# One branch for two groups of products, with up to four widths, in the first mixture of experts

## The chip, the core and the metric

The kernel runs on one core of a Trainium2 chip. Its engines work side by side and wait for each other through semaphores: TensorE (PE; its weight loads are shown as PEld), VectorE (DVE), ScalarE (ACT), GpSimd (POOL) and SyncE (SP). The metric is the device time of one execution in microseconds (us). The median of three runs before the change is 817.31 us (816.48 to 819.75).

## The reference

The kernel computes a chain of three layers in float32. The first is windowed attention (4 batches, 8 heads, 576 positions, head width 64). The second is a mixture of 8 experts over 2304 tokens, in which each token goes to the one expert that its gate picks. The third is a dense layer with a softplus. The second layer is where the change lies:

```
logits = x @ w_gate
e_idx = np.argmax(logits, axis=1)
...
for e in range(E):
    mask = e_idx == e
    h = np.maximum(x[mask] @ w1[e], 0.0)
    ye = h @ w2[e]
    out[mask] = gate_w[mask, None] * eom[mask, e, None] * ye
```

Here x is 2304x512, w1[e] is 512x1024 and w2[e] is 1024x512. How many tokens an expert gets is known only when the kernel runs.

## The kernel before, in words

Up to about 160 us the kernel does attention and the gate. Then it goes through the experts one after the other, as "ranks" 0 to 7 (`for r in range(NE)`, L1309): rank 0 is the expert that leads after the first 11 of 20 token tiles, and ranks 1 to 7 are the others by falling count. The second dense layer follows from about 396 us.

Each rank has a fixed capacity of columns (tokens), CAPS = 424, 392, 344, 328, 312, 288, 280, 256. Tokens beyond a capacity are done by `overflow()`, a block that all engines run past between rank 0 and rank 1; with the reference's inputs none is left over. Working out the reference's gate on its inputs gives 356, 370, 312, 309, 280, 278, 203 and 196 tokens for ranks 0 to 7.

A rank has 16 steps, u = 0 to 15. In steps 0 to 7, `up` computes one block of 128 hidden rows each (tile ph, with ReLU by ACT into hh and the rest hl by DVE). In steps 8 to 15, `down` computes four blocks of 128 output rows (tile py), each in two halves. A float32 product is split into high and low parts, so each term is three matmuls (wh xh, wh xl, wl xh). A group is the 12 matmuls of one `up` or of one half of a `down`; a rank has 16 groups, 192 matmuls.

PE, ACT, DVE and SP take their instructions in the order in which the code writes them (`manual_schedule`). In a step stand also, in this order: gathering and transposing the next rank's tokens (`gather_tr`, PE transposes into px, L855, two buffers), splitting a weight piece into its high and low part (`hi_` on ACT, `lo_` on DVE), and then `up` or `down`. The weights come by DMA (tile wr); a new load is issued by SP as soon as `lo_` has freed a buffer.

Matmuls need not run over the whole capacity. `mm3_r` (L871) reads the rank's token count from a register of PE and branches: if the count is at most the rank's cut in CUTS (L26), the group runs over the cut's columns (L890 to L892; the first matmul of an accumulation stays as wide as the capacity), else over the capacity (L894 to L896). Rank 0 has no branch. Each group has its own branch, and both forms ("arms") stand in PE's program one behind the other.

Of the kernel before, what the change touches and what calls it, by code (L numbers as in the profile page):

```python
# [11 lines left out]
F32 = mybir.dt.float32  # L12
# [9 lines left out]
P = 128  # L22

MASKED = 1.0e30
ROWS_AT = 8
CUTS = [(), (344,), (320,), (304,), (288,), (264,), (256,), (240,)]  # L26
RB = 5
WARM = 28
NE_AT = ((6, 14), (7, 0), (7, 1), (7, 2))
# [13 lines left out]
def attn_moe_softplus_kernel(ctx: ExitStack, tc: tile.TileContext, q, k, v, w_gate, w_ogate, w1, w2, w_in, w_out, out, dbg=None):  # L43
    nc = tc.nc
    B, H, S, D = q.shape
    NT, DM = out.shape
    NE = w_gate.shape[1]
# [6 lines left out]
    NC = DM // P  # L54
# [24 lines left out]
    tabi = const.tile([1, 40], I32, name="tabi")  # L79
# [453 lines left out]
    K = {"rt": rt_p, "ixe": const}  # L533
# [292 lines left out]
    def part(r, j, c, n, fs):  # L826
        return [t.rearrange("p (c f) -> p c f", c=n)[:, c, fs] for t in pieces[r, j][-2:]]
# [38 lines left out]

    rows_val = {}

    def mm3_r(r, n, ps, terms, *a):
        if r not in rows_val:  # L870
            mm3(ps[:, :n], [(w, [x[:, :n] for x in xs_]) for w, xs_ in terms], *a)  # L871
            return

        def arms(cuts):
            if not cuts:
                mm3(ps[:, :n], [(w, [x[:, :n] for x in xs_]) for w, xs_ in terms], *a)
                return
            with tc.If(rows_val[r] <= cuts[0]) as c:
                mm3(ps[:, :n], [(w, [x[:, :n] for x in xs_]) for w, xs_ in terms], *a, cut=cuts[0])
            with c.Else():  # L880
                arms(cuts[1:])

        arms(CUTS[r])

    def mm3(ps, terms, first=True, last=True, cut=None):
        k = len(terms)
        for i, ((wh, wl), (xh, xl)) in enumerate(terms):
            if cut:
                wide = first and i == 0
                nc.tensor.matmul(ps if wide else ps[:, :cut], wh, xh if wide else xh[:, :cut], start=wide, stop=False, skip_group_check=True)  # L890
                nc.tensor.matmul(ps[:, :cut], wh, xl[:, :cut], start=False, stop=False, skip_group_check=True)  # L891
                nc.tensor.matmul(ps[:, :cut], wl, xh[:, :cut], start=False, stop=(last and i == k - 1), skip_group_check=True)  # L892
                continue
            nc.tensor.matmul(ps, wh, xh, start=(first and i == 0), stop=False)  # L894
            nc.tensor.matmul(ps, wh, xl, start=False, stop=False)  # L895
            nc.tensor.matmul(ps, wl, xh, start=False, stop=(last and i == k - 1))  # L896

    hT = {}

    def up(r, n, f):  # L900
        xh, xl = xs[r]
        pool, tag = K["ph"]
        ps = pool.tile([P, 512], F32, tag=tag, name=f"ph{r}_{f}")
        fs = slice(P * (f % 2), P * (f % 2) + P)
        mm3_r(r, n, ps, [(part(r, f // 2, c, 4, fs), (xh[:, c], xl[:, c])) for c in range(NC)])
        hh, hl = [K["hh"].tile([P, CW], F32R, tag=t, name=f"{t}{r}_{f}") for t in ("hh", "hl")]
        nc.scalar.activation(hh[:, :n], ps[:, :n], AF.Relu)
        nc.vector.scalar_tensor_tensor(hl[:, :n], ps[:, :n], 0.0, hh.bitcast(F32)[:, :n], ALU.max, ALU.subtract)
        hT[r, f] = (hh[:, :n], hl[:, :n])

    yps = {}
# [9 lines left out]
                tc.declare_no_dep(ywr[r, o].ins, ld.ins, reason="this rank lies behind the columns read")  # L921

    def down(r, n, o, half, off, eng):
        if half == 0:
            yps[r, o] = K["py"][0].tile([P, 512], F32, tag=K["py"][1], name=f"py{r}_{o}")
        ps = yps[r, o]
        os_ = slice(P * o, P * o + P)
        fs = range(4 * half, 4 * half + 4)
        mm3_r(r, n, ps, [(part(r, 4 + f // 2, f % 2, 2, os_), hT[r, f]) for f in fs], half == 0, half == 1)
        if half == 1:  # L930
            store_y(r, n, o, ps, off, eng)

    NL = GROUPS[G_DRAM][1]
    xacc = {}
# [301 lines left out]
        K[key] = (bctx.enter_context(tc.tile_pool(name=nm, bufs=bufs, space=PSUM)), nm)  # L1239
    def overflow():  # L1240
        total = nc.values_load(tabi[0:1, 4 * NE : 4 * NE + 1], min_val=0, max_val=NT // OVW)
        with tc.If(total > 0):


            with tc.For_i(0, NE) as r:
                left = nc.values_load(tabi[0:1, ds(r + 3 * NE, 1)], min_val=0, max_val=NT // OVW)
                with tc.For_i(0, left) as kw:
                    e_, o_, c_ = [
                        nc.sync.value_load(tabi[0:1, ds(r + i * NE, 1)], min_val=0, max_val=m)
                        for i, m in ((0, NE - 1), (1, NT), (2, NT))  # L1250
                    ]
                    t0 = nc.s_assert_within(c_ - kw * OVW - OVW, min_val=0, max_val=NT - OVW, skip_runtime_bounds_check_because="an overflow window ends at its expert's last token")
                    y0 = nc.s_assert_within(o_ + t0, min_val=0, max_val=NT - OVW, skip_runtime_bounds_check_because="an overflow window ends at its expert's last token")
                    load_idx("v", e_ * NT + t0, OVW)
                    for t in range(ntile(OVW)):
                        gather("v", OVW, t)
                    for j in range(4):
                        load_piece("v", j, e_)
                        piece_hi("v", j)
                        piece_lo("v", j)  # L1260
                    for t in range(ntile(OVW)):
                        for fn in (gather_scale, gather_tr, gather_hi, gather_lo):
                            fn("v", OVW, t)
                    for f in range(NF1):
                        up("v", OVW, f)
                    for j in range(4, 8):
                        load_piece("v", j, e_)
                        piece_hi("v", j)
                        piece_lo("v", j)
                    for o in range(NC):  # L1270
                        for half in range(2):
                            down("v", OVW, o, half, y0, nc.sync)
# [43 lines left out]
    for r in range(NE):  # L1316
        n = CAPS[r]
        if r == 1:
            sched.close()
            overflow()  # L1320
            mctx.enter_context(tc.manual_schedule(engines=manual))
        off = tab_load(nc.scalar, NE + r, NT) if r else 0
        perm_off = tab_load(nc.sync, NE + r, NT) if r else 0
        nc.sync.dma_start(perm_dram[ds(perm_off, NT)], idx_dram[ds(er[r] * NT, NT)])
        for u in range(16):

            if r == 0:
                next(ordering, 0)
                if u == ROWS_AT:
                    loaded = nc.values_load_multi_w_load_instructions(tabi[0:1, 2 * NE + 1 : 3 * NE], engines=[nc.tensor.engine])[1]  # L1330
                    rows_val.update({k_ + 1: v_ for k_, v_ in enumerate(loaded)})
                if u == 4:
                    K["ranked"] = True
                    er[1] = tab_load(nc.sync, 1, NE - 1)
                    load_idx(1, er[1] * NT, CAPS[1])
                    nload[1] -= 1
                    load_next()
            if r + 2 < NE:
                if u == IDX_AT:
                    if r + 2 not in er:  # L1340
                        er[r + 2] = tab_load(nc.sync, r + 2, NE - 1)
                    load_idx(r + 2, er[r + 2] * NT, CAPS[r + 2])
                if 0 <= u - GATHER_AT < ntile(CAPS[r + 2]):
                    gather(r + 2, CAPS[r + 2], u - GATHER_AT)
            if r + 1 < NE:
                m = CAPS[r + 1]
                if r == 0 and 0 <= u - 6 < ntile(m):
                    gather(r + 1, m, u - 6)
                for s, fn in zip((9, 10, 11, 12) if r == 0 else TR_AT, (gather_scale, gather_tr, gather_hi, gather_lo)):
                    if 0 <= u - s < ntile(m):  # L1350
                        fn(r + 1, m, u - s)

            if r < NE - 1 or u < 8:
                k_ = (r, 4 + u // 2) if u < 8 else (r + 1, (u - 8) // 2)
                (hi_, lo_)[u % 2](*k_)
            if r == NE - 1:
                for fn, *a in last_rank.get(u, ()):
                    fn(*a)
            if (r, u) in NE_AT:
                load_piece(NE, NE_AT.index((r, u)))  # L1360
            if r == NE - 1:
                if u in X2_AT:
                    x2_load(X2_AT.index(u))
            if r and u % 5 == 0:
                prep_tick(new_b, NPREP, 3)
            if u < 8:
                up(r, n, u)
            else:
                down(r, n, (u - 8) // 2, u % 2, off, nc.scalar)
# [154 lines left out]
```

## Time and profile before

| what | value |
|---|---|
| median of 3 runs | 817.31 us (816.48 to 819.75) |
| the profiled execution, its own time | 819.59 us |
| its span, first to last instruction | 818.0 us |
| PE matmul busy | 773.8 us, 95% |
| PE weight loads busy | 694.5 us, 85% |
| DVE / ACT / POOL busy | 566.6 / 471.8 / 144.6 us |
| ranks 0 to 7 | about 160 to 396 us |
| mean granted clock of PE | 0.986 |

All times in the profile are of one execution. A matmul's shown duration holds its passage through the array, so back-to-back matmuls overlap in the timeline; what one costs the stream is the distance between the starts.

### The profile page before, as it was taken

The numbers are of one execution on the slowest core, as the hardware profiler recorded it, in microseconds if no ns is written. First come the engines' busy times: TensorE is split into PE (matmuls) and PEld (weight loads), VectorE is DVE, ScalarE is ACT, GpSimd is POOL, SyncE is SP. The second block draws the span as 40 slices with busy tenths as digits, with TensorE's granted clock in tenths as the row PEclk, the third lists the DMA queues.
The fourth block names the chain that finished last, engine by engine and source line by source line (L and its number), as shares of the span: only waits on it lengthen the run. The fifth ranks groups of instructions, "written<-read, shape, count | busy, mean of one in ns | idle before, by whom it ended". The sixth has DMA issues, their size and how long they took to land.

```text
span 818.0 us, 14909 instructions
## 1 busy us (share of the span) xinstructions
PE 773.8 (95%) x5542; PEld 694.5 (85%) x5543; DVE 566.6 (69%) x1112; ACT 471.8 (58%) x909; POOL 144.6 (18%) x170
## 2 busy tenths in 40 slices
PE   6898886999999999999989999999999999999994
PEld 5666664898999999999978887899999999999993
DVE  5767885663667877756799999866656666766662
ACT  4675642344556666566766666656656655655561
POOL 9824343121002012100011222120001001001001
PEclk9999998799999999999999999999999999999998
DMA  9997665255788898669432312220001001001000
GB/s 209 264 243 186 144 159 154 59 193 182 233 275 277 304 299 279 213 216 320 135 103 78 104 53 83 70 85 1 20 0 40 1 1 39 1 0 40 1 1 38
DMA packets 85879, 104.36 MB, mean 128 GB/s; under 512 B 30428, under 2 KB 61404, under 8 KB 85792
## 3 DMA queue, kind: packets, MB, share of 16 engines
q1 hardware_dynamic: 74496, 84.22, 35.7%
q0 software_dynamic: 5104, 13.40, 4.9%
q10 hardware_dynamic: 6192, 5.56, 2.0%
q8 instruction: 57, 0.93, 0.5%
q14 instruction: 30, 0.25, 0.1%
HBM read 83.98 MB, written 19.32 MB: 126 GB/s over the span
## 4 chain that ended last, share of the span: by engine, by line
PE 59%; DVE 12%; issue 9%; ACT 4%; DMA 2%; POOL 1%; POOLq 0%; ACTq 0%; SPq 0%; DVEq 0%
PE pg L895 5%; PE pg L896 5%; PE pg L894 5%; PE q L1433 5%; PE q L1432 5%; PE q L1431 5%; PE ph L894 3%; PE ph L896 3%; PE py L894 3%; PE ph L895 3%; PE py L895 2%; PE py L896 2%; DVE l L1411 2%; PE py L890 2%; PE py L891 2%
## 5 line engine op out<-in xcount | busy, mean ns | idle before, releaser
L895 PE MATMUL pg<-xlm,wh 128*128 128x384 f32 x384 | 129.7, 338 | 0.0
L896 PE MATMUL pg<-xhm,wl 128*128 128x384 f32 x384 | 129.4, 337 | 0.0
L894 PE MATMUL pg<-xhm,wh 128*128 128x384 f32 x384 | 129.4, 337 | 0.0
L1433 PE MATMUL q<-wh,gl 128*128 128x512 f32 x288 | 114.2, 397 | 3.8 <-DVE gl L732 3.8
L1431 PE MATMUL q<-wh,gh 128*128 128x512 f32 x288 | 114.2, 396 | 1.3 <-ACT gh L1417 0.9
L1432 PE MATMUL q<-wl,gh 128*128 128x512 f32 x288 | 113.3, 393 | 0.0
L732 DVE TENSOR_TENSOR wl<-wr,wh 128x1024 fp32r<-128x1024 f32 x72 | 87.6, 1219 | 33.3 <-ACT wh L787 33.3
L1417 ACT CAST gh<-l 128x384 fp32r<-128x384 f32 x96 | 49.2, 513 | 100.5 <-DVE l L1411 100.5
L732 DVE TENSOR_TENSOR gl<-l,gh 128x384 fp32r<-128x384 f32 x96 | 56.6, 590 | 41.3 <-ACT gh L1417 40.2
L787 ACT CAST wh<-wr 128x1024 fp32r<-128x1024 f32 x72 | 75.0, 1047 | 15.2 <-ACT y L917 6.7
L894 PEld LDWEIGHTS pg<-xhm,wh 128*128 128x128 f32 x384 | 72.2, 188 | 3.9
L895 PEld LDWEIGHTS pg<-xlm,wh 128*128 128x128 f32 x384 | 72.1, 188 | 3.8
L1433 PEld LDWEIGHTS q<-wh,gl 128*128 128x128 f32 x288 | 54.1, 188 | 21.9 <-DVE gl L732 10.2
L1402 DVE TENSOR_SCALAR w<-u 128x384 f32<-128x384 f32 x96 | 34.7, 361 | 54.6 <-ACT u L1400 53.9
L896 PEld LDWEIGHTS pg<-xhm,wl 128*128 128x128 f32 x384 | 72.2, 188 | 0.0
L1440 POOL DMA_INDIRECT out_dram<-o,perm_sb x18 | 18.6, 1033 | 271.9 <-DVE o L259 137.4
L1411 DVE TENSOR_TENSOR l<-l,u 128x384 f32<-128x384 f32 x96 | 62.2, 648 | 2.8
L1431 PEld LDWEIGHTS q<-wh,gh 128*128 128x128 f32 x288 | 54.1, 188 | 11.7 <-ACT gh L1417 4.2
L1432 PEld LDWEIGHTS q<-wl,gh 128*128 128x128 f32 x288 | 54.1, 188 | 8.2
L1399 ACT ACTIVATE u<-pg 128x384 f32<-128x384 f32 x96 | 46.9, 489 | 22.9 <-PE pg L896 22.5
L837 POOL DMA_INDIRECT xg<-x_dram,idx x25 | 29.9, 1198 | 167.7 <-ACT wh L787 79.0
L1404 DVE SCALAR_TENSOR_TENSOR u<-w,u 128x384 f32<-128x384 f32 x96 | 53.5, 557 | 2.8
(205 smaller groups left out, 1806.8 us busy)
## 6 DMA issues: line engine op xcount, KB each, us to landing
wr<-in_moe_w_dram SPq DMA_DIRECT2D x64, 512.0 KB, 5.4
raw<-in_q_dram SPq DMA_DIRECT2D x8, 576.0 KB, 7.0
raw<-in_k_dram SPq DMA_DIRECT2D x8, 576.0 KB
x2r<-yT_dram SPq DMA_DIRECT2D x12, 384.0 KB, 4.6
vP<-in_v_dram SPq DMA_DIRECT2D x16, 272.0 KB, 10.8
praw<-in_moe_w_in_dram SPq DMA_DIRECT2D x8, 512.0 KB
praw<-in_moe_w_out_dram SPq DMA_DIRECT2D x8, 512.0 KB, 5.8
wr<-in_moe_w_in_dram SPq DMA_DIRECT2D x8, 512.0 KB
```

Of the source, the lines that this page charges most:

```text
L732: e.tensor_tensor(lo, src, hi.bitcast(F32), ALU.subtract)
L787: (eng or nc.scalar.copy)(d[1], d[0])
L894: nc.tensor.matmul(ps, wh, xh, start=(first and i == 0), stop=False)
L895: nc.tensor.matmul(ps, wh, xl, start=False, stop=False)
L896: nc.tensor.matmul(ps, wl, xh, start=False, stop=(last and i == k - 1))
L1399: nc.scalar.activation(u, ps, AF.Abs)
L1404: nc.vector.scalar_tensor_tensor(u, w_, 1.0, u, ALU.subtract, ALU.subtract)
L1411: nc.vector.tensor_tensor(l, l, u, ALU.subtract)
L1417: nc.scalar.copy(gT[b, f][0], l)
L1431: nc.tensor.matmul(acc[b, t], gh[:, ts_], wh, start=(f == 0), stop=False)
L1432: nc.tensor.matmul(acc[b, t], gh[:, ts_], wl, start=False, stop=False)
L1433: nc.tensor.matmul(acc[b, t], gl[:, ts_], wh, start=False, stop=(f == NF - 1))
```

## The change

Three edits, all of which act on PE's program.

1. `mm3_r` takes several groups and puts one branch around them. `up` now issues the groups of steps f and f+1 together in the even step, and `down` both halves together in its first step (the second step only stores).
2. CUTS gets up to three cuts for a rank, tried in rising order, so that four forms of each pair of groups stand in the program. Rank 0 gets cuts too: the register load moves from step 8 to step 10 of rank 0 and now holds rank 0's count, so its outputs o = 1 to 3 (the last six groups) branch.
3. The overflow test is turned round (`total <= 0` with an empty body, else the loop) and gets a label; a prefetch hint for that branch is written in step 14 of rank 0, for PE.

```diff
-ROWS_AT = 8
-CUTS = [(), (344,), (320,), (304,), (288,), (264,), (256,), (240,)]
+ROWS_AT, HINT_AT = 10, 14
+CUTS = [(328, 360, 392), (328, 352, 372), (304, 316, 328), (288, 300, 312), (264, 280, 296), (248, 260, 272), (240, 256), (240,)]
...
+    def mm3_r(r, n, groups):
+        def plain():
+            for ps, terms, *a in groups:
+                mm3(ps[:, :n], [(w, [x[:, :n] for x in xs_]) for w, xs_ in terms], *a)
 
         def arms(cuts):
             if not cuts:
-                mm3(ps[:, :n], [(w, [x[:, :n] for x in xs_]) for w, xs_ in terms], *a)
+                plain()
                 return
             with tc.If(rows_val[r] <= cuts[0]) as c:
-                mm3(ps[:, :n], [(w, [x[:, :n] for x in xs_]) for w, xs_ in terms], *a, cut=cuts[0])
+                for ps, terms, *a in groups:
+                    mm3(ps[:, :n], [(w, [x[:, :n] for x in xs_]) for w, xs_ in terms], *a, cut=cuts[0])
             with c.Else():
                 arms(cuts[1:])
 
-        arms(CUTS[r])
+        arms(CUTS[r] if r in rows_val else ())
...
+        if f % 2 == 0:
+            groups = []
+            for g in (f, f + 1):
+                phs[g] = pool.tile([P, 512], F32, tag=tag, name=f"ph{r}_{g}")
+                fs = slice(P * (g % 2), P * (g % 2) + P)
+                groups.append((phs[g], [(part(r, g // 2, c, 4, fs), (xh[:, c], xl[:, c])) for c in range(NC)]))
+            mm3_r(r, n, groups)
...
+            for h in range(2):
+                fs = range(4 * h, 4 * h + 4)
+                groups.append((ps, [(part(r, 4 + f // 2, f % 2, 2, os_), hT[r, f]) for f in fs], h == 0, h == 1))
+            mm3_r(r, n, groups)
...
-        with tc.If(total > 0):
+        with tc.If(total <= 0, label="overflow", preferred_fallthrough_block=False) as none_left:
+            pass
+        with none_left.Else():
...
+                if u == HINT_AT:
+                    tc.mark_branch_hint_location("overflow", "LikelyTaken", engines=[nc.tensor.engine])
                 if u == ROWS_AT:
-                    loaded = nc.values_load_multi_w_load_instructions(tabi[0:1, 2 * NE + 1 : 3 * NE], engines=[nc.tensor.engine])[1]
-                    rows_val.update({k_ + 1: v_ for k_, v_ in enumerate(loaded)})
+                    loaded = nc.values_load_multi_w_load_instructions(tabi[0:1, 2 * NE : 3 * NE], engines=[nc.tensor.engine])[1]
+                    rows_val.update({k_: v_ for k_, v_ in enumerate(loaded)})
```

PE's program grows from 5858 to 8216 rows. What stands where shows at three places.

On PE in rank 1, at the end of the `up` steps, this stands before (ph1 is an `up` block of rank 1, px2 a transpose for rank 2):

```order
L878 UNCONDITIONAL_BRANCH
L855 MATMUL px2_0_3606<-identf_64,xg2_0_2845 128x128 x4
L878 COMPARE_AND_BRANCH
L890 MATMUL ph1_7_3614<-xh1_2797,wh1_3_2902 128x392
L891 MATMUL ph1_7_3614<-xl1_2798,wh1_3_2902 128x344
L892 MATMUL ph1_7_3614<-xh1_2797,wl1_3_2903 128x344
```

And this at the same place in the program now (py1_0 is the first `down` block):

```order
L878 UNCONDITIONAL_BRANCH
L855 MATMUL px2_0_4056<-identf_64,xg2_0_2922 128x128 x4
L855 MATMUL px2_1_4079<-identf_64,xg2_1_3035 128x128 x4
L878 COMPARE_AND_BRANCH
L891 MATMUL py1_0_4088<-hh1_0_3699,wh1_4_3587 128x392
L892 MATMUL py1_0_4088<-hl1_0_3700,wh1_4_3587 128x328
L893 MATMUL py1_0_4088<-hh1_0_3699,wl1_4_3588 128x328
```

A transpose that stood between the seventh and the eighth `up` group now stands behind the eighth, next to the following transpose; the order of the groups themselves is as it was.

On PE in rank 1, second `down` block, this stands now between the second form of the pair and the third, each of 24 matmuls:

```order
L891 MATMUL py1_1_4215<-hh1_7_4064,wh1_7_3945 128x352
L892 MATMUL py1_1_4215<-hl1_7_4065,wh1_7_3945 128x352
L893 MATMUL py1_1_4215<-hh1_7_4064,wl1_7_3946 128x352
L878 UNCONDITIONAL_BRANCH
L878 COMPARE_AND_BRANCH
L891 MATMUL py1_1_4215<-hh1_0_3699,wh1_4_3587 128x392
L892 MATMUL py1_1_4215<-hl1_0_3700,wh1_4_3587 128x372
```

Before, a compare led to one of two forms of 12 matmuls; now PE's sequencer compares up to three times and jumps over up to three forms of 24.

At the head of PE's program (both programs, the change with its signs):

```order
-L1509 ISA
-L1519 UNCONDITIONAL_BRANCH
+L1520 ISA
+L1530 UNCONDITIONAL_BRANCH
+L1530 BRANCH_PREFETCH_HINT
 L97 LDWEIGHTS zeros
 L97 MATMUL warm<-zeros 128x144
```

The hint written in step 14 of rank 0 stands ahead of PE's first matmul in the program that was built.

## Rows read from the trace of the kernel before

**Rows 1.** The page, part 1: busy time, share of the span, instructions.

```profile
PE 773.8 (95%) x5542; PEld 694.5 (85%) x5543; DVE 566.6 (69%) x1112; ACT 471.8 (58%) x909; POOL 144.6 (18%) x170
```

**Rows 2.** Busy time by stretch: window, length, engines, PE clock, DMA share, GB/s.

```profile
200.00:236.00 36.00, 35.32 (x203) 35.24 (x204) 18.63 (x26) 18.68 (x29) 3.15 (x3) 1.00 0.72 240
236.00:267.00 31.00, 31.00 (x215) 30.90 (x215) 24.00 (x37) 19.05 (x31) 4.54 (x3) 1.00 0.89 277
267.00:296.00 29.00, 29.00 (x198) 28.72 (x197) 21.78 (x34) 17.92 (x29) 3.59 (x3) 1.00 0.91 304
296.00:323.00 27.00, 27.00 (x205) 26.78 (x204) 21.89 (x34) 18.00 (x30) 4.26 (x3) 1.00 0.87 276
323.00:350.00 27.00, 26.87 (x205) 26.46 (x204) 19.73 (x31) 16.02 (x27) 2.63 (x2) 1.00 0.73 238
350.00:373.00 23.00, 23.00 (x197) 23.00 (x196) 13.04 (x18) 14.64 (x24) 0.00 (x0) 1.00 0.64 204
373.00:396.00 23.00, 22.95 (x202) 22.71 (x201) 15.28 (x20) 14.88 (x25) 0.00 (x0) 1.00 1.00 314
...
500.00:800.00 300.00, 299.25 (x1502) 270.28 (x1501) 200.27 (x388) 178.52 (x385) 21.52 (x19) 1.00 0.07 23
```

**Rows 3.** Waits of PE, 158 to 405 us: total us, times, longest.

```profile
PE ph L894 <- DVE xl L732: 1.2, 1, 1.2
PE ph L894 <- ACT y L917: 0.7, 1, 0.7
PE px L855 <- DVE xl L732: 0.2, 1, 0.2
```

**Rows 4.** Waits of PE, 405 to 818 us.

```profile
PE q L1433 <- DVE gl L732: 3.8, 9, 0.8
PE q L1431 <- ACT gh L1417: 0.9, 2, 0.6
```

**Rows 5.** Waits of ACT, 200 to 396 us, the longest entry.

```profile
ACT y L917 <- PE py L896: 19.6, 12, 2.6
```

**Rows 6.** PE's timeline in rank 0, 424 columns: start, duration, instruction.

```profile
161.22 0.36 PE L894 MATMUL ph<-xh,wh 128*128 128x424 f32 x1
...
178.92 0.35 PE L896 MATMUL ph<-xh,wl 128*128 128x424 f32 x1
```

**Rows 7.** PE's timeline in rank 1, 392 columns, with a transpose.

```profile
201.11 0.34 PE L896 MATMUL ph<-xh,wl 128*128 128x392 f32 x1
...
215.55 0.34 PE L896 MATMUL ph<-xh,wl 128*128 128x392 f32 x1
215.73 0.60 PE L855 MATMUL px<-identf,xg 128*128 128x128 f32 x4
216.09 0.43 PE L894 MATMUL ph<-xh,wh 128*128 128x392 f32 x1
216.35 0.34 PE L895 MATMUL ph<-xl,wh 128*128 128x392 f32 x1
```

**Rows 8.** PE's timeline in rank 7, 240 columns.

```profile
384.75 0.27 PE L891 MATMUL py<-hl,wh 128*128 128x240 f32 x1
...
385.98 0.27 PE L890 MATMUL py<-hh,wh 128*128 128x240 f32 x1
```

**Rows 9.** Timeline around the overflow test, between rank 0 and rank 1.

```profile
199.59 0.35 PE L896 MATMUL py<-hh,wl 128*128 128x424 f32 x1
199.98 0.51 ACT L917 COPY y<-py 128x424 f32<-128x424 f32 x1 [2.59 <-PE py L896]
...
200.68 0.42 PE L894 MATMUL ph<-xh,wh 128*128 128x392 f32 x1 [0.73 <-ACT y L917]
```

**Rows 10.** DMA: a queue's packets, MB, share; issues with KB and us to landing.

```profile
q8 instruction: 57, 0.93, 0.5%
...
wr<-in_moe_w_dram SPq DMA_DIRECT2D x64, 512.0 KB, 5.4
...
perm_dram<-idx_dram SPq DMA_DIRECT2D x8, 18.0 KB, 3.5
```

More of the change, by code (lines that the diff above doesn't have):

```diff
@@ L867, in attn_moe_softplus_kernel @@
     rows_val = {}
-    def mm3_r(r, n, ps, terms, *a):
-        if r not in rows_val:
-            mm3(ps[:, :n], [(w, [x[:, :n] for x in xs_]) for w, xs_ in terms], *a)
-            return
+    def mm3_r(r, n, groups):
+        def plain():
+            for ps, terms, *a in groups:
+                mm3(ps[:, :n], [(w, [x[:, :n] for x in xs_]) for w, xs_ in terms], *a)
         def arms(cuts):
             if not cuts:
-                mm3(ps[:, :n], [(w, [x[:, :n] for x in xs_]) for w, xs_ in terms], *a)
+                plain()
                 return
             with tc.If(rows_val[r] <= cuts[0]) as c:
-                mm3(ps[:, :n], [(w, [x[:, :n] for x in xs_]) for w, xs_ in terms], *a, cut=cuts[0])
+                for ps, terms, *a in groups:
+                    mm3(ps[:, :n], [(w, [x[:, :n] for x in xs_]) for w, xs_ in terms], *a, cut=cuts[0])
             with c.Else():
                 arms(cuts[1:])
-        arms(CUTS[r])
+        arms(CUTS[r] if r in rows_val else ())
     def mm3(ps, terms, first=True, last=True, cut=None):
@@ L898, in attn_moe_softplus_kernel @@
     hT = {}
+    phs = {}
     def up(r, n, f):
@@ L902, in up @@
         pool, tag = K["ph"]
-        ps = pool.tile([P, 512], F32, tag=tag, name=f"ph{r}_{f}")
-        fs = slice(P * (f % 2), P * (f % 2) + P)
-        mm3_r(r, n, ps, [(part(r, f // 2, c, 4, fs), (xh[:, c], xl[:, c])) for c in range(NC)])
+        if f % 2 == 0:
[5 more added lines that the diff above has]
+            mm3_r(r, n, groups)
+        ps = phs[f]
         hh, hl = [K["hh"].tile([P, CW], F32R, tag=t, name=f"{t}{r}_{f}") for t in ("hh", "hl")]
@@ L923, in down @@
     def down(r, n, o, half, off, eng):
+        os_ = slice(P * o, P * o + P)
         if half == 0:
[L925 to L931, printed above, removed]
+            yps[r, o] = ps = K["py"][0].tile([P, 512], F32, tag=K["py"][1], name=f"py{r}_{o}")
+            groups = []
+            for h in range(2):
+                fs = range(4 * h, 4 * h + 4)
+                groups.append((ps, [(part(r, 4 + f // 2, f % 2, 2, os_), hT[r, f]) for f in fs], h == 0, h == 1))
+            mm3_r(r, n, groups)
+        else:
+            store_y(r, n, o, yps[r, o], off, eng)
     NL = GROUPS[G_DRAM][1]
```

## The prediction

> **What bounds the kernel now.** I read the busy table first, then the stretches of the ranks, then PE's waits, then PE's timeline in three ranks, and last the DMA table. The busy table gives PE 95% of the span [rows 1]. [...] The waits agree: from 158 to 405 us PE idles three times, 2.1 us together [rows 3], and from there to the end 4.7 us [rows 4]. The other engines wait for PE: ACT's copies of the outputs alone wait 19.6 us [rows 5]. So a microsecond taken from PE's stream in the ranks should come off the end, as long as nothing else holds PE back by then. DMA is nearest to that: its share is 0.87 to 0.91 in ranks 2 to 4 and 1.00 in rank 7 [rows 2].
>
> **What a column costs.** The starts of matmuls give their price. At 424 columns 92 steps take 178.92 - 161.22 = 17.70 us, 192.4 ns each [rows 6]; at 392 columns 81 steps take 14.44 us, 178.3 ns [rows 7]; at 240 columns 11 steps take 1.23 us, 111.8 ns [rows 8]. From 424 to 240 that is 80.6 ns for 184 columns, 0.438 ns a column. It is even over the whole range (424 to 392 gives 0.44), so narrower matmuls are not held up by their weight loads here, nor by the branches that stand in ranks 1 and 7 after every 12 matmuls and that leave no gap in these rows.
>
> **The change part by part.**
>
> *Widths.* With the token counts of the reference, each rank's width goes from and to: rank 0 (356) 424 to 360, in its last three output blocks only; rank 1 (370) 392 to 372; rank 2 (312) 320 to 316; rank 3 (309) 328 to 312; rank 4 (280) 288 to 280; rank 5 (278) stays at 288, as its largest cut is 272; rank 6 (203) 256 to 240; rank 7 (196) stays at 240. A rank has 192 matmuls, of which the first of each of its 12 accumulations stays at the capacity, so 180 get narrower; in rank 0 it is 72 less 3, 69. Columns saved: 69x64 + 180x(20 + 4 + 16 + 8 + 16) = 4416 + 11520 = 15,936. At 0.438 ns this is 6.98 us, all in a stream that PE fills.
>
> *Order on PE.* The groups keep their order, so weights, hh and hl are wanted at the same points as before, and a pair's second group waits at its own first matmul, not at the head of the form. What moves is the transposes of odd steps, 12 matmuls later. The splits that read them stand on ACT and DVE behind work that waits for the same 12 matmuls, so I cost the delay at nothing; if that cover fails, one split and its wait (0.5 to 1 us of PE) is the price in a rank. Two things come back. In seven places two transposes now stand together, and the first matmul behind a transpose takes 0.26 us to the next where 0.18 is usual [rows 7]: 7 x 0.08 = 0.56 us saved. And the one wait of a transpose for DVE, 0.2 us [rows 3], gets 12 more matmuls of cover: 0.2 us saved.
>
> *The register load of rank 0* moves from step 8 to step 10 and now stands directly before the branch that needs it. PE's sequencer issues ahead of the array (the load at step 8 left no gap among rank 0's waits [rows 3]), so nothing; at worst it drains PE once, like the overflow test below, 0.9 us.
>
> *The overflow test.* Between rank 0 and rank 1 PE goes from a start at 199.59 to one at 200.68 us, 1.09 us where 0.19 is usual: 0.9 us lost [rows 9]. ACT's last copy of rank 0 starts and ends inside this gap. Past the test PE first waits for its own earlier matmuls and for DVE to have passed its own test, and neither changes. So the hint, if it works, gains between 0 and 0.9 us; I take 0, since the gap looks like a drain and not like a late fetch. Behind it rank 1 now needs three compares before its first matmul, with an empty array in front: two more, for which no row has a price; from 0 to the 0.9 us of the whole test, I take 0.2 us lost. [...]
>
> *Sum.* 6.98 + 0.56 + 0.2 - 0.2 = 7.5 us. The profiled execution took 819.59 us and would take 812.1; it lay 2.3 us over the median of the runs, 817.31, which would become **809.8 us**.
>
> **Rivals.**
>
> *1. The far jump stalls PE at the overflow test.* The jump over the overflow block is as long as before, but rank 1's first form is no longer the one that runs: its third is, some 100 instructions further on, and PE's array is empty there, so a late fetch shows at once. Against it stands the hint; but the hint is the first instruction of PE's program, some 200 us ahead of its branch, and may have no effect so early. The price lies between 0 and one landing of a block of code; the nearest row in size is the copy of 18 KB, 3.5 us [rows 10]. That gives 809.8 + 3.5 = 813.3 us.
>
> *2. PE's sequencer is bound by the fetch of its code (the slower side).* PE's instructions come in 57 packets, 0.93 MB together [rows 10], or 16 KB each. Counting each product with its weight load, as PE and PEld do, the program of before has some 14,750 PE instructions, about 260 a packet. Before, a pair of groups takes 4x24 instructions and the branches, some 0.4 packet; with four forms of 48 it takes about 204 instructions, 0.785 packet, of which one form is run and three are jumped over. Ranks 1 to 5 then need 8 x 0.785 = 6.3 packets each. Their times after the change would be about 33.7, 29.7, 28.5, 26.4 and 27 us (their stretches [rows 2] less the columns), so a packet every 4.2 us is fast enough everywhere. At 5.0 us a packet a rank takes 31.4 us and ranks 2 to 5 lose 1.7, 2.9, 5.0 and 4.4; rank 6, with three forms (4.7 packets, 23.5 us against 22), loses 1.5: 15.5 us, giving 825.3 us. At 5.4 it would be 838. For it: DMA is at 0.87 to 0.91 just in ranks 2 to 4 [rows 2], where a 512 KB weight load takes 5.4 us to land [rows 10]. Against it: a code packet is 16 KB, and the 18 KB copies land in 3.5 us; and the fetch may run more than one packet ahead. It decides from about 4.2 us, and eats the whole gain at about 4.7.
> The trace shows code arriving in 57 packets but no stall by one [rows 3, 10]. [...]
>
> *3. The gain is taken back by the weights.* DMA's share is 1.00 in rank 7 [rows 2]. If that stretch can't start earlier, rank 6's own 1.3 us is lost, 811.1 us. Against it: loads are issued when `lo_` frees a buffer, so they move forward with PE, and in rank 6 the share is only 0.64.
>
> **How the numbers follow.** The forecast gets 0.56: 808 to 812 us by the bounds above (0.9 us each for the test and the load, and the transposes). Rival 1 gets 0.20 at 813.3, rival 2 0.17 at 825 (a spread from 814 to 838), rival 3 0.07 at 811. The range that leaves out no more than 2 in 10 runs from 807.5 to 818 us; what it leaves out is most of rival 2. Half a per cent, about what a measurement of this kernel can tell from no change, is 4.1 us: faster means under 813.2. The forecast and rival 3 lie there, and half of rival 1: 0.56 + 0.06 + 0.10 = 0.72. Within half a per cent lie the other half of rival 1 and rival 2 at 4.5 to 4.9 us a packet, 0.16. Slower is the rest of rival 2, 0.12.
>
> **What would show it.** In the changed profile the matmuls of rank 0's last three blocks should start 164 ns apart, rank 1's 170, rank 3's 143, rank 4's 129, rank 6's 112, and PE's waits in the ranks should stay near 2 us. The second layer should begin about 7.5 us earlier and last as long as before. Rival 1 shows as a gap of over 2 us ahead of rank 1's first matmul, with all other engines done. Rival 2 shows as gaps of PE in ranks 2 to 5 whose releaser is "issue", every pair or so, worst in ranks 4 and 5. Rival 3 shows as PE waiting for DVE's weight splits in rank 7. The forecast is wrong if PE's waits in the ranks grow by more than 3 us, or if the second layer gets longer by what the first one lost.

## The result and the profile after

The change made the kernel slower: 823.43 us (median of 22 runs) against 818.55 us for the kernel before on the same chip, a ratio of 1.0065 (95% interval 1.0051 to 1.0079). The forecast was 809.8 us, its range ended at 818. The profiled execution has a span of 820.8 us against 818.0.

The busy table answers to [rows 1]:

```profile
PE 770.6 (94%) x5542; PEld 690.0 (84%) x5543; DVE 567.5 (69%) x1112; ACT 472.8 (58%) x909; POOL 141.5 (17%) x170
```

PE has 3.2 us less work and yet ends 2.8 us later. The stretches of ranks 1 to 7, and the second layer, answer to [rows 2] (window, length, PE, PEld, DVE, ACT, POOL, PE clock, DMA share, GB/s):

```profile
197.40:232.10 34.70, 34.35 (x204) 34.03 (x205) 18.65 (x26) 18.29 (x28) 3.27 (x3) 1.00 0.73 238
232.10:261.30 29.20, 29.20 (x207) 29.19 (x206) 22.61 (x35) 18.68 (x30) 4.65 (x3) 1.00 0.90 272
261.30:294.00 32.70, 30.85 (x205) 30.34 (x205) 22.69 (x36) 18.45 (x30) 2.79 (x3) 0.95 0.86 291
294.00:325.00 31.00, 27.36 (x206) 26.22 (x204) 23.07 (x37) 18.70 (x31) 2.80 (x3) 1.00 0.83 265
325.00:353.80 28.80, 27.63 (x205) 26.86 (x206) 19.90 (x29) 15.95 (x27) 1.91 (x2) 1.00 0.66 209
353.80:376.40 22.60, 22.60 (x201) 22.60 (x201) 12.86 (x19) 14.83 (x24) 0.00 (x0) 1.00 0.64 205
376.40:398.60 22.20, 22.00 (x194) 21.76 (x193) 14.61 (x20) 14.60 (x24) 0.00 (x0) 1.00 1.00 325
500.00:800.00 300.00, 299.29 (x1500) 270.08 (x1499) 201.60 (x392) 178.16 (x385) 21.53 (x19) 1.00 0.07 23
```

Ranks 1, 2, 6 and 7 are filled as before. In ranks 3, 4 and 5 PE is idle for 1.85, 3.64 and 1.17 us, and rank 3 has a clock of 0.95. The second layer is as it was. PE's waits from 155 to 415 us answer to [rows 3]:

```profile
PE py L891 <- issue: 2.0, 2, 1.2
PE ph L891 <- ACT wh L787: 1.9, 1, 1.9
PE ph L891 <- ACT y L925: 1.5, 1, 1.5
PE ph L895 <- DVE xl L732: 1.2, 1, 1.2
PE ph L895 <- DVE pw L178: 0.9, 1, 0.9
PE ph L891 <- DVE pw L178: 0.9, 1, 0.9
PE ph L895 <- ACT y L925: 0.5, 1, 0.5
PE ph L891 <- DVE wl L732: 0.3, 1, 0.3
...
PE py L892 <- DVE hl L916: 0.2, 1, 0.2
```

Together 9.8 us (two entries of 0.2 us, both "issue", are left out) where there were 2.1. The names on the right change from line to line, and some can't be right: no `up` product reads pw (it belongs to the second layer's weights), and the wh that ends at such a moment is a piece for `down`. It looks as if the last event that happens to lie near is named when nothing that PE waits for is in the profile. Two of the waits in PE's timeline, one in rank 3 between two `up` pairs, one in rank 4 between transposes and a `down` pair (start, duration, instruction):

```profile
264.57 0.30 PE L893 MATMUL ph<-xh,wl 128*128 128x312 f32 x1
266.73 0.42 PE L891 MATMUL ph<-xh,wh 128*128 128x328 f32 x1 [1.85 <-ACT wh L787]
266.98 0.32 PE L892 MATMUL ph<-xl,wh 128*128 128x312 f32 x1
...
268.08 0.46 PE L893 MATMUL ph<-xh,wl 128*128 128x312 f32 x1
268.34 0.46 PE L891 MATMUL ph<-xh,wh 128*128 128x312 f32 x1
...
271.54 0.31 PE L892 MATMUL ph<-xl,wh 128*128 128x312 f32 x1
...
308.36 0.82 PE L855 MATMUL px<-identf,xg 128*128 128x128 f32 x6
310.07 0.40 PE L891 MATMUL py<-hh,wh 128*128 128x312 f32 x1 [0.89 <-issue]
```

About 1.1 us behind the first wait the steps from one matmul's start to the next grow from 0.14 to 0.26 us. The windows of the wait and of what follows it show why: the granted clock, 1.00 in the first, is 0.50 in the second, from 267.9 to 271.2 us.

```profile
264.60:266.70 2.10, 0.27 (x2) 0.01 (x1) 2.10 (x4) 1.66 (x3) 0.00 (x0) 1.00 1.05 374
267.90:271.20 3.30, 3.30 (x14) 3.30 (x13) 1.37 (x2) 0.44 (x1) 0.00 (x0) 0.50 0.95 353
```

Fourteen matmuls at 260 instead of 143 ns are 1.6 us more, on top of the wait. The overflow test, answering to [rows 9]: from one matmul's start to the next 1.83 us, where it was 1.09.

```profile
195.59 0.32 PE L893 MATMUL py<-hh,wl 128*128 128x360 f32 x1
...
197.42 0.42 PE L891 MATMUL ph<-xh,wh 128*128 128x392 f32 x1 [1.51 <-ACT y L925]
```

And the row of the DMA table that answers to [rows 10] has 75 packets of code for 57:

```profile
q8 instruction: 75, 1.23, 0.6%
```

### The profile page after: what moved, and what is told of

Its sections match the earlier page's. It is cut to its first block, busy times and chain, and to the rows that moved or that the text cites. A ratio compares the mean times of both kernels' runs of the same rounds, so it can differ in the third digit from the quotient of the medians.

```text
span 820.8 us, 14902 instructions
## 1 busy us (share of the span) xinstructions
PE 770.6 (94%) x5542; PEld 690.0 (84%) x5543; DVE 567.5 (69%) x1112; ACT 472.8 (58%) x909; POOL 141.5 (17%) x170
## 4 chain that ended last, share of the span: by engine, by line
PE 60%; DVE 12%; issue 9%; ACT 5%; DMA 2%; POOL 0%; SPq 0%; POOLq 0%; ACTq 0%; DVEq 0%
PE q L1444 5%; PE pg L896 5%; PE pg L897 5%; PE pg L895 5%; PE q L1443 5%; PE q L1442 5%; PE py L891 3%; PE py L892 3%; PE py L893 3%; PE ph L891 3%; PE ph L893 3%; PE ph L892 3%; DVE l L1422 2%; DVE l L1420 1%; PE ph L895 1%
## 5 line engine op out<-in xcount | busy, mean ns | idle before, releaser
L891 PE MATMUL py<-hh,wh 128*128 128x312 f32 (+10 forms) x216 | 66.6, 308 | 2.0 <-issue 2.0
L892 PE MATMUL py<-hl,wh 128*128 128x240 f32 (+5 forms) x216 | 65.1, 301 | 0.2 <-DVE hl L916 0.2
L893 PE MATMUL py<-hh,wl 128*128 128x240 f32 (+5 forms) x216 | 65.0, 301 | 0.0
L891 PE MATMUL ph<-xh,wh 128*128 128x392 f32 (+5 forms) x192 | 58.8, 306 | 4.6 <-ACT wh L787 1.9
```

## The experiments

These rows leave three theories. **F**: PE's sequencer waits for its code (rival 2 of the prediction). **C**: the failing compares and the jumps cost the time by themselves. **W**: pairs and moved transposes make PE wait for ACT and DVE. "Ranks" below is the time from rank 0's first product to the second layer's first product in the profiled execution: 235.3 us before, 239.9 after the change. Ratios are to the kernel before on the same chip, with 95% intervals. In the traces of the first four runs (two_forms to five_forms) rank 0 starts at 170 to 175 us, in all others at 155 to 162 us, and the kernel before took 829.09 us beside them; so ratios and "ranks" are compared, not times.

**two_forms.** One fitting cut a rank: the widths that run are those of the change, with half the code.

```diff
+CUTS = [(360,), (372,), (316,), (312,), (280,), (288,), (240,), (240,)]
```

> The change, but with one cut a rank, the fitting one: the widths that run are those of the change, one compare stands ahead of a pair, and two forms instead of four stand in the code. Theory F (PE's sequencer is held up by the fetch of its code): a rank has 8 x 0.4 = 3.2 packets of code, far under what 22 to 39 us allow, so the stalls of ranks 3 to 5 go and the gain of the widths shows: about 811 to 813 us, 6 to 7 below before. Theory C (the failing compares and the jumps from form to form cost the time): the same. Theory W (one branch for two groups and the moved transposes make PE wait for ACT and DVE): pairs and transposes are as in the change, so it stays at about 823.

Measured: 0.9896 (0.9864 to 0.9929), ranks 228.6 us. The gain is there with pairs, moved transposes and hint in place. W falls.

**three_forms, fit_first, five_forms.** The fitting form first, then one, two or three forms that are never run:

```diff
+CUTS = [(360, 392), (372, 380), (316, 328), (312, 320), (280, 296), (288, 288), (240, 256), (240,)]
+CUTS = [(360, 376, 392), (372, 376, 380), (316, 320, 328), (312, 316, 320), (280, 284, 296), (288, 288, 288), (240, 256), (240,)]
+CUTS = [(360, 376, 392, 400), (372, 376, 380, 384), (316, 320, 328, 336), (312, 316, 320, 324), (280, 284, 296, 304), (288, 288, 288, 288), (240, 256, 264), (240, 248)]
```

> As two_forms, with one more form a pair in ranks 0 to 6 that is never run, the fitting form first, so still one compare a pair. F: a rank has 8 x 0.59 = 4.7 packets; at about 4.5 us a packet that is 21 us, still under the 26 us of the shortest rank with three forms: 811 to 813 us, as two_forms. C: as two_forms, 811 to 813. W: 823.

> Four forms a pair as in the change, the same length of code, but the fitting form is the first, so one compare a pair that never fails, and one long jump over three forms. F: the same 6.3 packets a rank as the change, so stalls in ranks 3 to 5 come back: 816 to 823 us. C: one compare, so 811 to 813. W: 823, whatever the order.

> As fit_first, with a fifth form that is never run in ranks 0 to 6 (four in 6, three in 7). F: a rank has 8 packets, 36 us at 4.5 us a packet, against 28 to 35 us of matmuls in ranks 2 to 5: these lose 5 to 9 us each, 840 to 850 us in all. C: 811 to 813, since one compare stands in each pair. W: 823.

| forms a pair | packets of code | ranks, us | ratio |
|---|---|---|---|
| 2 (two_forms) | 56 | 228.6 | 0.9896 |
| 3 (three_forms) | 66 | 231.6 | 0.9956 (0.9928 to 0.9984) |
| 4 (fit_first) | 75 | 235.2 | 1.0031 (1.0005 to 1.0057) |
| 5 (five_forms) | 86 | 262.8 | 1.0325 (1.0292 to 1.0358) |

The same matmuls and one compare a pair in all four: the time rises with code that is not run. Failing compares can't do that, F asks for it. By size F missed once: three forms, expected free, lose 2.9 us in the ranks, 1.1 of them at the overflow test. Rank by rank, this is what each loses against two_forms, in us (the overflow test counts in rank 0; the change's loss in rank 3 and those of five_forms in ranks 1, 5 and 7 hold falls of the granted clock to 0.50, fit_first's hold none):

| | 0 | 1 | 2 | 3 | 4 | 5 | 6 | 7 |
|---|---|---|---|---|---|---|---|---|
| two_forms takes | 37.8 | 34.1 | 29.1 | 29.1 | 26.6 | 27.2 | 22.7 | 22.0 |
| three_forms loses | 1.1 | 0 | 0 | 0 | 0.8 | 0 | 1.0 | 0 |
| fit_first loses | 0 | 0 | 0 | 3.7 | 1.5 | 0 | 1.1 | 0.2 |
| the change loses | 0.9 | 0.6 | 0 | 3.7 | 4.4 | 1.5 | 0 | 0.2 |
| five_forms loses | 1.4 | 2.2 | 5.6 | 5.9 | 5.2 | 7.6 | 2.4 | 3.9 |

So code that is not run is enough for a loss, but it is not the whole account of the change. fit_first has the same 75 packets and loses 6.6 us, the change 11.3. Whether the other 4.7 us come from the failing compares, which fit_first lacks, or from where in the code a block of it ends, is not shown. The losses don't follow the number of failing compares (two a pair in rank 3, one in rank 4, three in rank 5), and rank 6, which has the same forms in the same order in both, loses 1.1 us in fit_first and nothing in the change.

In fit_first PE even stops inside a form, as its timeline shows, at a product whose tiles (xh and wl) the product three places earlier has read already:

```profile
282.05 0.30 PE L893 MATMUL ph<-xh,wl 128*128 128x312 f32 x1
282.20 0.30 PE L891 MATMUL ph<-xh,wh 128*128 128x312 f32 x1
282.33 0.30 PE L892 MATMUL ph<-xl,wh 128*128 128x312 f32 x1
283.70 0.30 PE L893 MATMUL ph<-xh,wl 128*128 128x312 f32 x1 [1.06 <-issue]
283.84 0.30 PE L891 MATMUL ph<-xh,wh 128*128 128x312 f32 x1
```

Now the packets of code (count, MB, share) from 240 to 380 us. In two_forms:

```profile
q8 instruction: 17, 0.28, 0.8%
```

In the change:

```profile
q8 instruction: 29, 0.48, 1.4%
```

In five_forms, where waits run through ranks 2 to 5:

```profile
q8 instruction: 33, 0.54, 1.7%
```

With five forms a packet comes every 140 / 33 = 4.2 us, with waits all through: I take that for the rate at which the fetch binds. In the change one came every 4.8 us on the average, its waits counted in. What its ranks need is more: 6.3 packets (the prediction's estimate) in the 29.1, 26.6 and 27.2 us that ranks 3 to 5 take in two_forms are one every 4.6, 4.2 and 4.3 us, just at that rate. But rank 4 of three_forms needs only one every 5.7 us (4.7 packets in 26.6 us) and still loses 0.8 us, while rank 2 of the change, with one every 4.6 us, loses nothing. So a need below the average rate was no guarantee, and the spare time of rank 3 in three_forms (4.7 packets in 29.1 us, no loss) did not carry PE through rank 4. Two windows of five_forms show that the packets are uneven, 6 in 29 us (4.8 us each) at a DMA share of 0.84 and 4 in 14 us (3.5) at 0.64:

```profile
293.00:322.00 29.00, 24.07 (x165) 22.90 (x166) 19.47 (x31) 14.88 (x24) 2.79 (x3) 1.00 0.84 266
322.00:336.00 14.00, 13.10 (x102) 12.59 (x100) 10.62 (x17) 9.03 (x16) 0.00 (x0) 1.00 0.64 198
```

**four_early.** Four forms with the change's cuts where a rank is long (0 to 2), two in ranks 3 to 7:

```diff
+CUTS = [(328, 360, 392), (328, 352, 372), (304, 316, 328), (312,), (280,), (288,), (240,), (240,)]
```

> Ranks 0 to 2 as in the change (four forms, cuts tried in rising order, one or two of which fail), ranks 3 to 7 with the one fitting cut. F (fetch of code): at the 4.2 us a packet that five_forms showed, 6.3 packets need 27 us, and ranks 1 and 2 have 34 and 29 us, so they do not stall except at the overflow test (1 us more); ranks 3 to 7 have 3.2 packets. About as two_forms: 7 to 8 us below before. Theory C (failing compares cost time by themselves): half of the failing compares of the change stand in ranks 0 to 2, so about half of its loss stays: 3 to 5 us below before at most. Theory K (the loss is in the whole length of the program, wherever the forms stand): packets are between two_forms and the change, so a loss of some 5 us against two_forms.

Measured: 0.9950 (0.9931 to 0.9968), ranks 230.3 us, 64 packets. By time it lies 4.1 us (the ratio) or 5.0 us (the medians, 813.47 and 818.43) below before, where F gave 7 to 8, C 3 to 5, and K a loss of some 5 against two_forms: the time alone speaks for C or K. Where the 1.7 us against two_forms lie speaks against both: 1.1 at the overflow test (a step of 2.05 us for 0.90), 0.2 each in ranks 1 and 7; rank 2 is the same (29.1 us). So the failing compares of ranks 1 and 2 cost 0.3 us at most, and the stalls of ranks 3 to 5 go when the extra forms there go. Their failing compares go with them, so this run alone does not part the two.

**four_single.** The kernel before with the change's cuts for ranks 1 to 7: no pairs, no branch in rank 0, no hint.

```diff
+CUTS = [(), (328, 352, 372), (304, 316, 328), (288, 300, 312), (264, 280, 296), (248, 260, 272), (240, 256), (240,)]
```

> The pairs undone and the four forms kept: the kernel before with the change's cuts for ranks 1 to 7, a branch for each group of 12, no branch in rank 0, no hint. The code of a rank is as long as in the change (16 x 102 instructions, 6.4 packets), each jump half as far. Theory F (packets per time): ranks 3 to 5 stall as in the change; 5 us gained by the columns, 9 to 12 lost: 4 to 7 above before. Theory J (a single jump must be long to cost something: three forms of 24 are, three of 12 are not): no stalls, 4 to 5 below before.

Measured: 1.0062 (1.0038 to 1.0086), ranks 241.7 us, 75 packets: as slow as the change, with jumps half as long. fit_single (below) is the same kernel with two forms and takes 231.1 us in the ranks, so the two further forms cost 10.6 us, 8.7 of them in ranks 3 to 5. J falls: a single jump need not be long.

**quiet_fetch.** two_forms with code that is never run in the fourth block of the second layer, where DMA's share is 0.03 (`twelve` writes the 12 matmuls of one group of its second product):

```diff
+        if b == 3:
+            with tc.If(rows_val[7] <= 256) as c_:
+                mm3(ps, terms)
+            with c_.Else():
+                for _ in range(9):
+                    mm3(ps, terms)
...
+        if b == 3 and 0 < f < NF - 1:
+            with tc.If(rows_val[7] <= 256) as c_:
+                twelve()
+            with c_.Else():
+                for _ in range(10):
+                    twelve()
```

> two_forms with code that is never run inside the second layer, where hardly any other data moves: in its fourth block of tokens each group of 12 matmuls jumps over nine or ten copies of itself, some 24 packets of code in about 64 us of matmuls, a packet every 2.7 us. Theory L (a packet takes 4.2 us because other transfers are in its way): here it takes about 3 us, the block 70 to 80 us, 10 to 15 us lost. Theory R (4.2 us is the fetch's own round trip): the block takes about 100 us, 35 to 40 us lost.

Measured: 1.0087 (1.0054 to 1.0120); ranks 228.6 us as in two_forms, the second layer 14.5 us longer (411.5 to 426.0). The packets of code from 610 to 682 us:

```profile
q8 instruction: 22, 0.36, 2.0%
```

And the busy times of the same window:

```profile
610.00:682.00 72.00, 61.04 (x290) 51.12 (x290) 37.16 (x73) 34.26 (x75) 0.00 (x0) 1.00 0.03 9
```

A packet every 72 / 22 = 3.3 us at a DMA share of 0.03, against 4.2 at 0.74 (the mean from 240 to 380 us in five_forms). So R falls, and code costs time outside the experts too. That the weights' traffic is what makes the fetch about a quarter slower there fits these two cases but is not shown: they differ in their code as well, and in five_forms itself packets came 4.2 us apart (9 in the 38 us from 358 us on) at a share of 0.56.

**no_hint and hint_alone.** two_forms without the hint (the edit below); the kernel before with the turned test and the hint only (part 3 of the change).

```diff
-                if u == HINT_AT:
-                    tc.mark_branch_hint_location("overflow", "LikelyTaken", engines=[nc.tensor.engine])
```

> two_forms without the hint for the overflow branch. Theory N (the hint does nothing so early in the program): time as two_forms, 7 to 9 us below before, and PE's gap at the overflow test near 0.7 us as there. Theory H (the hint fetches the target): the gap grows by 1 to 4 us, 4 to 8 us below before.

> The kernel before with the turned overflow test and its hint alone. no_hint had a gap of 2.6 us at the test and two_forms 0.7, the kernel before 0.9. Theory M (the hint hides a late fetch where there is one, and before there was none): no change, 0 to 0.3 us. Theory T (it saves a fixed piece of every far jump): 1 to 2 us below before, the gap near zero.

Measured: no_hint 0.9951 (0.9938 to 0.9965), ranks 230.4 us; hint_alone 0.9998 (0.9979 to 1.0016), ranks 235.3 us. PE around the test in no_hint:

```profile
194.12 0.32 PE L893 MATMUL py<-hh,wl 128*128 128x360 f32 x1
196.84 0.42 PE L891 MATMUL ph<-xh,wh 128*128 128x392 f32 x1 [2.40 <-PEq L1249]
```

And with the hint, in two_again (below):

```profile
192.04 0.32 PE L893 MATMUL py<-hh,wl 128*128 128x360 f32 x1
192.94 0.42 PE L891 MATMUL ph<-xh,wh 128*128 128x392 f32 x1 [0.58 <-ACT y L925]
```

2.72 against 0.90 us, and the hint is all that differs: it is worth 1.8 us here, though it stands at the head of the program. In the kernel before it does nothing. That it works by fetching the target early is argued and not shown, and it is no remedy everywhere: with the same hint in place the step at the test is 2.02 us in three_forms, 2.30 in five_forms and 2.05 in four_early, and 0.90 in fit_first. These steps don't follow the compares ahead of it either, one in three_forms, five_forms and fit_first, three in four_early.

**fit_single, tight, two_again.** The kernel before with the fitting cuts alone; two_forms with tighter cuts; two_forms a second time, on the chip of four_single.

```diff
+CUTS = [(), (372,), (316,), (312,), (280,), (288,), (240,), (240,)]
...
+CUTS = [(360,), (372,), (312,), (312,), (280,), (280,), (208,), (200,)]
```

> The kernel before with the fitting cuts alone: each group of 12 has its own branch as before, two forms of 12, no branch in rank 0, no hint. Theory V (the widths alone give the gain): 64 x 180 = 11,520 columns at 0.438 ns, 5.0 us below before. Theory B (a branch for each group costs PE time that one for two groups saves): under 4 us below before, as two_forms would owe part of its 8 us to the pairs.

> As two_forms with cuts as near to the counts as steps of 8 or 4 allow: rank 2 316 to 312, rank 5 288 to 280, rank 6 240 to 208, rank 7 240 to 200. 180 x (4 + 8 + 32 + 40) = 15,120 columns less than two_forms, at 0.438 ns 6.6 us. Theory S (price per column even below 240 columns): 6 us faster than two_forms, 14 to 15 below before. Theory D (rank 7 is bound by its weights' transfers, and a weight load sets a floor below 240 columns): ranks 6 and 7 gain little, at most 2 to 3 us against two_forms, 10 to 11 below before.

> The kernel of two_forms a second time, beside hint_alone and four_single. By the traces (the ranks took 6.7 us less than before) 6 to 7.5 us below before; 8.5 as in its first timing if that was no chance.

Measured: fit_single 0.9953 (0.9938 to 0.9969), ranks 231.1 us; tight 0.9913 (0.9897 to 0.9930), ranks 227.7; two_again 0.9908 (0.9884 to 0.9932), ranks 228.6. The widths of ranks 1 to 7 alone give 3.9 us by the ratio (4.2 in the ranks, 5.0 expected). In the traces two_again takes 2.2 us less than fit_single in rank 0, where its branches and the hint act, and 0.2 us less in ranks 1 to 7, so the pairs bring next to nothing and B falls, though 3.9 alone would have left it standing. tight takes 15,120 columns away and gains 1.0 us in the ranks, 0.7 of it in ranks 2 and 5. In ranks 6 and 7 a step is as long at 200 or 208 columns as at 240, within 2 ns. Rank 7 in tight:

```profile
371.18 0.27 PE L891 MATMUL ph<-xh,wh 128*128 128x200 f32 x1
...
371.85 0.27 PE L891 MATMUL ph<-xh,wh 128*128 128x200 f32 x1
```

And in two_again:

```profile
365.92 0.27 PE L892 MATMUL ph<-xl,wh 128*128 128x240 f32 x1
...
366.59 0.28 PE L892 MATMUL ph<-xl,wh 128*128 128x240 f32 x1
```

Six steps in 0.67 us, 112 ns each, in both. So next to nothing is to be had below 240 columns here. What sets the 112 ns no run shows.

## Why the prediction was wrong

**The step that failed** is the fetch of PE's code. The forecast's sum has no term for it, and rival 2, which had it, got a chance of 0.17 and a price that was an average: "a packet every 4.2 us is fast enough everywhere". The measured price is 11.3 us in the ranks, of which the length of the code alone accounts for 6.6 (fit_first); what the other 4.7 come from stays open. Rival 2's mechanism is what came, with the signs named for it (gaps in ranks 3 to 5, some with "issue" as releaser). Its size was taken wrong at two points.

*The fetch's own time.* I held a landing time of 3.5 us of an 18 KB copy [rows 10] against it. The rate at which code really comes where it is short, 3.3 us a packet in quiet_fetch and 4.2 in five_forms, no row of before shows: there a rank needed 3 or 4 packets and the fetch never bound. I named the DMA share of 0.87 to 0.91 [rows 2] as a sign for the rival and did not price it.

*Averages.* At 4.2 us my sum lost nothing, yet the change lost about 12 us: its runs are 0.65% above before, two_again's 0.92% below, and 1.6% of 818 us is 12.8; in the ranks it is 239.9 - 228.6 = 11.3. By stretch the packets came 3.5 to 4.8 us apart in five_forms, the change needs one every 4.2 to 4.6 us in ranks 3 to 5, and PE stood still for up to 1.9 us at a time there. Two of the rank times in that sum are off as well: rows 2 less the columns give 30.7 and 27.7 us for ranks 2 and 3, not 29.7 and 28.5 (without stalls they measured 29.1 each). And at 4.2 us 6.3 packets take 26.4 us, so the sum stood at its edge in rank 4 (26.6 us). Ranks 4 and 5 were named as the worst; 3 and 4 were (3.7 and 4.4 us). In rank 3, 1.6 of the 3.7 us is the clock, which fell after the longest wait; the prediction had no term for that.

In the ranks PE waits 2.1 us in the kernel before (57 packets) and 1.8 us in two_forms (56), the wait at the overflow test counted in. From three forms on the cost of the code stands in the open: against two_forms the ranks take 2.9 us more with 66 packets, 6.6 with 75 and 34.2 with 86.

**What held.** *Widths*: 6.98 us forecast for the columns and 7.5 for all; with the code kept short two_again takes 6.7 us off the ranks and 0.92% (7.5 us) off the time. That 7.5 meets 7.5 is in part luck: the interval runs from 5.6 to 9.5 us. The periods came as said, within 1.5 ns. Ranks 1 and 6 gave less than their columns, 1.4 for 1.6 and 0.9 for 1.3 us; in rank 6 a step takes 112 ns at 240 columns and at 208 (tight), so that the 0.438 ns a column did not hold to the end of its range. *Order on PE*: no wait is left in the ranks of two_again but the one at rank 0's start and 0.6 us at the overflow test, so the moved transposes cost nothing. Of the 0.76 us that they were to give back 0.2 came (ranks 1 to 7 take 191.1 us in fit_single and 190.8 in two_again); the 0.56 for transposes that stand together did not. *Extra compares*: nothing forecast within the ranks; four_early agrees within 0.3 us a rank, where code is not short. At the test 0.2 us were forecast for two more compares, and no run shows that price: the step there took 1.83 us in the change with three compares, but 0.90 in two_again and 2.02 in three_forms with one each. *The register load*: nothing, as forecast. *The overflow hint* I took as 0; it is worth 0 in the kernel before and 1.8 us in two_forms. *Rival 1* was half right: the gap grew by 0.7 us and not by 3.5. *Rival 3* did not come up: rank 7 takes 22.0 us in two_again, at a DMA share of 1.02, and rank 6's gain was kept.

## What to carry to other kernels

Code that is jumped over can cost time: for the same matmuls the ranks took 228.6 us with 56 packets of code and 262.8 with 86. Count all the forms that stand in the program, divide by the time that the taken one runs, and compare that, stretch by stretch, with the rate of code packets (one every 3.3 to 4.2 us here). A rate that sufficed on the average did not suffice here, so leave a margin: 3.2 packets a rank were free, 4.7 cost 3 us in all and 6.3 cost 7 to 11. One well placed cut with two forms beat four forms here; it was placed knowing the token counts of these inputs, and how it does with other counts no run shows.

## What the runs showed of the hardware

- The rate of code packets was 3.3 us each with DMA at 0.03 and 4.2 us with DMA at 0.74; both in stretches with many waits for code (PE idle for 11.0 of 72 us in quiet_fetch and 17.4 of 140 us in five_forms).
- The waits that are put down to code here stood in the change under "issue" (2.0 us before `down` products) and under engines that had just finished (1.9 us under ACT's wh, 0.9 under DVE's pw, neither read by the `up` product that waited). The clearest sign was a product in the middle of a form that waited 1.06 us in fit_first, with tiles that an earlier product of the form had read already.
- Without the hint, which stands at the head of PE's program and some 190 us ahead of its branch, the step at the overflow test was 2.72 us, with it 0.90 us. In three other kernels it was 2.0 to 2.3 us with the hint.
- A stall had a second price: after 1.9 us of waiting in rank 3 the granted clock was 0.50 for 3.3 us. It did not fall after the other waits of the change (1.5 us and less). The length of the wait alone does not decide: in five_forms the clock fell so four times, each time behind a step of 1.8 to 2.8 us, and not behind three other steps of 2.3 to 2.4 us. What else decides stays open.
